# Part B's query, key and input turns moved to VectorE, with scores in eight 32x64 TensorE tiles

## The chip, the cores and the metric

The kernel runs on one core of a Trainium2 chip. The number that counts is the device time of one execution, in microseconds (us); it is given as the median of three runs. One further execution was taken with the hardware profiler, and all rows quoted below are from that one.

## The reference, cut to what matters

The program computes two independent parts and joins their outputs along the last axis. Part A is a sliding, dilated attention over 2048 tokens; the change does not touch its code. Part B is a recurrent attention: 2048 tokens are cut into 64 segments of 32, and each segment also reads 8 memory rows that the segment before it has written. So the 64 segments run strictly one after another.

```python
M, seg = (8, 32); H, Dh = (32, 192)
...
mem = mem0
for s in range(n_seg):                       # 64 segments
    xs = x[:, s * seg_len:(s + 1) * seg_len, :].copy()
    h = jnp.concatenate([mem, xs], axis=1)   # 40 rows of 640
    q = jnp.einsum('btd,dhe->bhte', h, Wq)   # k and v likewise
    ...
    scores = jnp.einsum('bhqe,bhke->bhqk', q, k) * scale
    scores = jnp.where(mask[None, None], scores, -1000000000.0)
    p = _softmax(scores, axis=-1)
    o = jnp.einsum('bhqk,bhke->bhqe', p, v)
    o = jnp.einsum('bhte,hed->btd', o, Wo)
    mem = o[:, :M, :].copy()
    outs.append(o[:, M:, :])
```

## The kernel before

Part A runs first, on all engines, for some 170 us. While it runs, SyncE's queue (SP, the one hardware DMA queue of the program) already loads a part of Part B's weights into SBUF, copies the rest into DRAM tiles in the form in which they will be streamed (`copy_streamed`), and copies the input x into a DRAM tile `xwindows`, 64 rows for each segment (`copy_windows`): 32 rows that the segment works on (the "main" rows: 8 memory rows and the first 24 tokens) and 32 rows "ahead", which hold the last 8 tokens of four neighbouring segments. These 8 last tokens need no memory, so their projections are made for four segments at once (`RENEW`, `turn_late`, the stored blocks `Lb`), one weight group at a time; a segment in which a group's turn comes makes two passes over its weights in place of one.

Part B's 32 heads are worked in four groups of 8 heads. For each of q, k and v and each group there are 1536 weight columns, and five row chunks of 128 rows (`dc`): one unit of 384 KB each. Wo is cut in 24 units of 320 KB. Most units stay in SBUF (`resident`); 24 of them (`STREAMED`: 8 of k, 6 of v, 10 of o) are fetched again in each segment from the DRAM copies, through a ring of six buffers (`wstream`).

A segment goes as follows on TensorE, whose order is written out by hand in `segment` (L659); ScalarE, VectorE and GpSimd are ordered by the scheduler of the tile layer:

- `project32` (L477): x is the stationary operand (128 rows by 32 tokens), weights stream past it, 384 columns in each of four column tiles of 32; five chunks give 20 matmuls in a pass.
- `to_sb` copies the 128x384 result from PSUM into SBUF as bf16. In it the partition holds a pair of heads and a token, and the columns hold the 384 features of the pair.
- `turn` (L495) turns it so that features lie on partitions: three 128x128 matmuls against the identity, into PSUM. `fill` then copies the result into `QT` or, in two halves, into `KT`, on ScalarE or VectorE. For the stored last tokens GpSimd copies from `Lb`.
- `scores` (L569): per group 16 matmuls of 128x64 (40 columns each) in two column tiles.
- `softmax`, `put_p`: VectorE and, for the exponential, ScalarE.
- `turn_p` (L603) turns the probabilities on TensorE, `mix` (L619) multiplies them with v in four row tiles of 32x128, 32 matmuls per group; four evacuations follow into `OT`.
- `project_out` (L633): 24 matmuls of 128x64 per group, 320 columns each, into `Y`.
- `memory_rows` (L645), at the segment's end: the 8 new memory rows of Y are turned on TensorE (after four `PAD` matmuls whose result is overwritten) and copied by VectorE into the x tile `HX` of the next segment.

x itself comes into `HX` by `load_x` (L467): one transposing DMA for each segment. PSUM has eight banks: three for `acc`, four for `ps_x` (turns, scores, mix), one for Y.

Of the kernel before, what the change touches and what calls it, by code (L numbers as in the profile page):

```python
# [7 lines left out]
FP32 = mybir.dt.float32  # L8
# [278 lines left out]
BLOCKS = 18  # L287
# [10 lines left out]
def part_b(ctx, tc, B_x, B_mem0, B_Wq, B_Wk, B_Wv, B_Wo, out, ident, n_seg, pre, nbuf, mid):  # L298
# [6 lines left out]
    w_in = {m: w.rearrange("(dc p) h e -> p dc (h e)", p=128) for m, w in (("q", B_Wq), ("k", B_Wk), ("v", B_Wv))}  # L305
# [4 lines left out]
    def unit_src(u):  # L310
        m, c, dc = u
        if m == "o":
            return wo_v[:, c]
        return w_in[m][:, dc, 1536 * c:1536 * c + 1536]
# [6 lines left out]
    def copy_streamed():  # L321

        order = [(m, g) for m, g in need]
        units = []
        for m, g in order:
            if m == "o":
                units += [("o", i, 0) for i in range(6 * g, 6 * g + 6) if i in STREAMED["o"]]
            else:
                units += [(m, g, dc) for dc in range(5) if m != "q" and dc in STREAMED[m][g]]
        for u in units:  # L330
            copied[u] = dpool.tile([128, unit_cols(u)], BF16, name="wcopy_%s%d_%d" % u)[:]
            nc.sync.dma_start(unit_tile(copied[u], u), unit_src(u))
# [19 lines left out]
    def load_resident(units, engs):  # L352
        for k, u in enumerate(units):
            engs[k % len(engs)].dma_start(unit_tile(res[u], u), unit_src(u))
# [8 lines left out]
    XW = dpool.tile([n_seg, 2 * SEG, Dm], BF16, name="xwindows")  # L363

    def copy_windows():

        rows = [(XW[0, 0:M], mem2[0:M]), (XW[0, M:SEG], x2[0:SEG - M])]
        for a, b in ((1, 49), (49, n_seg)):
            rows.append((XW[a:b, 0:SEG], x2[SEG * a - M:SEG * b - M].rearrange("(s n) d -> s n d", n=SEG)))
        groups = x2.rearrange("(t n) d -> t n d", n=SEG)[:, SEG - M:SEG]  # L370
        groups = groups.rearrange("(m k) n d -> k m n d", k=4)
        windows = XW[:].rearrange("(m k) n d -> k m n d", k=4)
        for r in range(4):
            for i in range(4):
                dst = windows[r][:, SEG + M * i:SEG + M * i + M]
                if i >= r:
                    rows.append((dst, groups[i]))
                else:
                    rows.append((dst[0:n_seg // 4 - 1], groups[i][1:n_seg // 4]))
                    rows.append((dst[n_seg // 4 - 1], groups[i][n_seg // 4 - 1]))  # L380
        for dst, src in rows:
            nc.sync.dma_start(dst, src)
# [14 lines left out]
    HXs = [xpool.tile([128, 5, 64], BF16, name=f"HX{i}") for i in range(2)]  # L397
# [5 lines left out]
    qk_sb = pool("b_qk", bufs=3)  # L403
# [3 lines left out]
    ps_x = pool("b_ps_x", bufs=4, space=PSUM)  # L407
# [32 lines left out]
    KT = cpool.tile([128, 4, 4, L], BF16, name="KT")  # L440
# [4 lines left out]
    free = [cpool.tile([128, 3, 4, M], BF16, name=f"Lb{i}") for i in range(BLOCKS)]  # L445
# [8 lines left out]
    for t in LV + [Vst]:  # L454
        nc.gpsimd.memset(t[:, 192:256], 0.0)

    copies = {"n": 0}
    S_, V_ = nc.scalar.copy, nc.vector.tensor_copy
    ENGINES = {"sb": {"q": (V_, S_, S_, S_), "k": (S_, S_, S_, S_)}, "late": (V_, V_, V_, V_),
               "QT": (S_, S_, S_, V_), "KT": (S_, S_, S_, S_), "V": (S_, V_, V_, S_), "LV": (V_, S_, S_, V_),  # L460
               "PT": (S_, V_, V_, V_)}

    def evacuate(dst, src):
        copies["n"] += 1
        (S_ if copies["n"] % 2 else V_)(dst, src)  # L465

    def load_x(s):  # L467
        if s < n_seg:
            nc.sync.dma_start_transpose(HXs[s % 2][:], XW[s])

    def main(s):
        return HXs[s % 2][:, :, 0:SEG]

    def ahead(s):
        return HXs[s % 2][:, :, SEG:2 * SEG]
# [19 lines left out]
    def turn(sb, chunks=(0, 1, 2)):  # L495
        pt = ps_x.tile([128, len(chunks), 4, 32], FP32, tag="x", name="pt")
        for k, c in enumerate(chunks):
            nc.tensor.matmul(pt[:, k], lhsT=sb[:, 128 * c:128 * c + 128], rhs=ident, start=True, stop=True)  # L498
        return pt

    def tokens(t):
        return t[:, 0:12 * L].rearrange("p (j c n) -> p j c n", c=3, n=L)

    def fill(copy, m, n0, n1, src):

        if m == "q":
            copy(tokens(QT)[:, :, :, n0:n1].rearrange("p j c n -> p c j n"), src)  # L507
            return
        fill_outer(copy, n0, n1, src[:, 0:3:2])
        fill_middle(copy, n0, n1, src[:, 1])  # L510

    def fill_outer(copy, n0, n1, src):
        copy(KT[:, :, 0:3:2, n0:n1].rearrange("p j c n -> p c j n"), src)  # L513

    def fill_middle(copy, n0, n1, src):
        copy(KT[0:64, :, 1, n0:n1], src[0:64])
        copy(KT[64:128, :, 3, n0:n1], src[64:128])  # L517

    def turn_late(sb, m, g, s, start):

        pt = turn(sb)
        for t in range(start, next_start(m, g, start)):
            rows = pt[:, :, :, M * (t % 4):M * (t % 4) + M]
            if t == s:
                if m == "k" and g == 0:
                    fill_middle(V_, 32, L, rows[:, 1])
                    fill_outer(S_, 32, L, rows[:, 0:3:2])
                else:
                    fill(S_, m, 32, L, rows)
            else:  # L530
                late[m, g, t] = free.pop(0)
                evacuate(late[m, g, t][:], rows)

    def project_qk(s, m, g):
        renew = s == 0 or f"{m}{g}" in RENEW[s % 4]
        Xs = [ahead(s), main(s)] if renew else [main(s)]
        ps = project32(Xs, m, g)
        sbs = [to_sb(p, c) for p, c in zip(ps, [ENGINES["late"][g], ENGINES["sb"][m][g]][2 - len(ps):])]

        def turn_ahead():  # L540
            if renew:
                turn_late(sbs[0], m, g, s, s)
            else:
                b = late.pop((m, g, s))
                fill(nc.gpsimd.tensor_copy, m, 32, L, b[:])
                free.append(b)

        def turn_main():
            if m == "k" and g == 0:
                fill_middle(V_, 0, 32, turn(sbs[-1], (1,))[:, 0])  # L550
                fill_outer(S_, 0, 32, turn(sbs[-1], (0, 2))[:])
            else:
                fill(ENGINES["QT" if m == "q" else "KT"][g], m, 0, 32, turn(sbs[-1])[:])

        return turn_ahead, turn_main
# [13 lines left out]
    def scores(g):  # L569
        Sps = ps_x.tile([128, 4, L], FP32, tag="x")  # L570
        for n in range(8):
            a, part = n // 2, n % 2
            for g2 in range(2):
                at = L * (3 * a + g2 + part)
                nc.tensor.matmul(Sps[64 * g2:64 * g2 + 64, a, :], lhsT=QT[:, at:at + 64],  # L575
                                 rhs=KT[:, a, ((0, 1), (3, 2))[g2][part], :], start=(n == 0), stop=(n == 7),
                                 tile_position=(0, 64 * g2))
        return Sps

    def softmax(Sps):  # L580
        t1 = one.tile([128, 4, L], FP32, tag="t1")
        nc.vector.scalar_tensor_tensor(out=t1[:], in0=Sps[:], scalar=scale,  # L582
# [20 lines left out]
    def turn_p(g):  # L603

        split = 2 if g == 3 else 1
        pt = ps_x.tile([128, 2, 128], FP32 if split > 1 else BF16, tag="x")
# [12 lines left out]
    def mix(g, PT):  # L619

        ps = [ps_x.tile([128, 3, L], FP32, tag="x", name=f"OTps{a}") for a in range(4)]
        plan = [(late, half, k, col) for late in range(2) for half in range(2)
                for k, col in (((0, 0), (1, 128)), ((2, 320), (1, 192)))[half]]
        for n, (late, half, k, col) in enumerate(plan):
            V = LV[g] if late else Vst
            for a in range(4):
                nc.tensor.matmul(ps[a][:, k, :], lhsT=V[32 * a:32 * a + 32, col:col + 128],  # L627
                                 rhs=PT[32 * a:32 * a + 32, late, half, :],
                                 start=(n == 0), stop=(n == len(plan) - 1), tile_position=(32 * a, 0))
        for a in range(4):  # L630
            evacuate(OT[:, 3 * L * a:3 * L * a + 3 * L], ps[a][:].rearrange("p k n -> p (k n)"))
# [13 lines left out]
    def memory_rows(s, Ysb):  # L645
        pt = ps_x.tile([128, 5, M], FP32, tag="x")
        for _ in range(PAD):
            nc.tensor.matmul(pt[:, 0, :], lhsT=ident, rhs=ident[:, 0:M], start=True, stop=True)
        for dc in (2, 0, 1, 3, 4):
            for gv in range(2):  # L650
                c0, c1 = max(128 * dc, 320 * gv), min(128 * dc + 128, 320 * gv + 320)
                if c0 < c1:
                    lo = c0 - 128 * dc
                    nc.tensor.matmul(pt[lo:lo + c1 - c0, dc, :], lhsT=Ysb[:, c0 - 320 * gv:c1 - 320 * gv],  # L654
                                     rhs=ident[:, 64 * gv:64 * gv + M], start=True, stop=True,
                                     tile_position=(0, lo))
        nc.vector.tensor_copy(HXs[(s + 1) % 2][:, :, 0:M], pt[:])  # L657

    def segment(s):  # L659
# [22 lines left out]
        both(tk[2])  # L682
        PT[1] = turn_p(1)
# [35 lines left out]
    load_x(0)  # L719
    for u in [(m, g, dc) for m, g in (("k", 0), ("k", 1), ("v", 0)) for dc in STREAMED[m][g]][:nbuf]:  # L720
        fetched[u] = fetch(u)
# [74 lines left out]
```

## Time and profile before

| | us |
|---|---|
| median of three runs | 1980.87 |
| lowest and highest run | 1975.70, 1982.82 |
| span of the profiled execution | 1976.8 |
| TensorE matmul busy | 1890.8 (96%) |
| VectorE busy | 1032.1 (52%) |
| ScalarE busy | 927.4 (47%) |
| GpSimd busy | 262.3 (13%) |
| SP's DMA queue, share of 16 engines' span | 91.3% |
| first matmul of Part B | 171.1 |

The busy times are sums over the whole program. A busy TensorE isn't one at its peak: the ends of matmuls are modelled, and overlapping matmuls in different tiles count once. The granted clock of TensorE was full (9 of 9 tenths shown) in all 40 slices. The profiled execution's span lies 4.1 us under the median of the runs and inside their spread of 7.1 us.

### The profile page before, as it was taken

How to read it: one execution, taken by the hardware profiler on the slowest of the kernel's cores; microseconds unless marked ns; L12 is line 12 of the kernel's file. 1: busy time of each engine (PE TensorE's matmuls, PEld its weight loads, DVE VectorE, ACT ScalarE, POOL GpSimd, SP SyncE). 2: the span in 40 equal slices, each digit the busy share in tenths (PEclk: the TensorE clock that was granted, in tenths of full speed). 3: DMA queues.
4: the chain of work that ended last, by engine and by line, in shares of the span. 5: the costliest groups of instructions: out<-in, count | busy, mean ns of one | idle time of the engine just before them, and what ended most of it. 6: DMA issues, size and time to landing. Idle time of an engine off the chain costs nothing.

```text
span 1976.8 us, 99618 instructions
## 1 busy us (share of the span) xinstructions
PE 1890.8 (96%) x43006; PEld 1221.6 (62%) x43006; DVE 1032.1 (52%) x3431; ACT 927.4 (47%) x2963; POOL 262.3 (13%) x1070
## 2 busy tenths in 40 slices
PE   8998899999999999999999999999999999999998
PEld 5665566666666666666666666666666666666665
DVE  4885454455444554455445554455445554555454
ACT  3554344444444454444444454444444444444443
POOL 2001011111111111111111111111111111111111
PEclk9999999999999999999999999999999999999999
DMA  9936999999999999999999999999999999999997
GB/s 332 298 111 227 341 324 312 327 326 326 324 321 324 322 328 315 329 319 331 326 318 322 329 330 314 325 315 316 327 328 324 327 327 315 338 325 329 315 328 262
DMA packets 278203, 621.62 MB, mean 314 GB/s; under 512 B 62089, under 2 KB 72329, under 8 KB 277449
## 3 DMA queue, kind: packets, MB, share of 16 engines
q1 hardware_dynamic: 272258, 609.17, 91.3%
q8 instruction: 337, 5.52, 1.1%
q0 software_dynamic: 5504, 6.07, 1.0%
q14 instruction: 104, 0.85, 0.1%
HBM read 602.01 MB, written 19.27 MB: 314 GB/s over the span
## 4 chain that ended last, share of the span: by engine, by line
PE 67%; DMA 17%; ACT 7%; DVE 6%; issue 2%; SPq 0%; ACTq 0%; POOL 0%; POOLq 0%; DVEq 0%
PE acc L485 31%; PE Y L641 17%; DMA t<-wcopy_k 7%; PE pt L498 7%; DMA t<-wcopy_o 6%; DMA t<-wcopy_v 4%; PE Sps L575 3%; PE pq L95 3%; PE OTps L627 3%; DVE prod L151 1%; ACT sb L712 1%; ACT OT L708 1%; PE pt L610 1%; ACT KT L513 1%; ACT t L588 1%
## 5 line engine op out<-in xcount | busy, mean ns | idle before, releaser
L485 PEld LDWEIGHTS <-HX 128*32 128x32 bf16 x19380 | 467.1, 96 | 283.8 <-issue 54.5
L641 PEld LDWEIGHTS <-OT 128*64 128x64 bf16 x6144 | 317.8, 110 | 137.0 <-ACT OT L465 25.0
L485 PE MATMUL acc<-t,HX 128*32 128x384 bf16 x4524 | 342.9, 328 | 19.0 <-DMA t<-wcopy_k 9.3
L641 PE MATMUL Y<-wres_o,OT 128*64 128x320 bf16 x3584 | 331.2, 302 | 9.9 <-DVE OT L465 5.1
L485 PE MATMUL acc<-wres_q,HX 128*32 128x384 bf16 x6460 | 333.6, 328 | 1.1 <-issue 0.7
L492 ACT CAST sb<-acc 128x384 bf16<-128x384 f32 x448 | 210.1, 478 | 152.0 <-PE acc L485 132.4
L641 PE MATMUL Y<-t,OT 128*64 128x320 bf16 x2560 | 266.7, 301 | 10.4 <-DMA t<-wcopy_o 8.8
L485 PE MATMUL acc<-wres_v,HX 128*32 128x384 bf16 x4520 | 251.7, 327 | 0.7 <-DMA wres_v<-in_B_Wv_dram 0.7
L485 PE MATMUL acc<-wres_k,HX 128*32 128x384 bf16 x3876 | 224.6, 327 | 0.3 <-DVE sb L492 0.3
L588 ACT ACTIVATE t<-t 128x160 f32<-128x160 f32 x256 | 86.4, 338 | 288.5 <-DVE t L587 284.5
L498 PE MATMUL pt<-ident,sb 128*128 128x128 bf16 x1938 | 182.4, 221 | 8.5 <-ACT KT L513 0.9
L582 DVE SCALAR_TENSOR_TENSOR t<-Sps,mask 128x160 f32<-128x160 f32 x256 | 82.9, 324 | 178.5 <-PE Sps L575 173.2
L465 ACT CAST OT<-OTps 128x120 bf16<-128x120 f32 x512 | 108.6, 266 | 140.4 <-PE OTps L627 139.2
L498 PEld LDWEIGHTS <-sb 128*128 128x128 bf16 x1938 | 109.4, 97 | 87.0 <-ACT sb L492 20.5
L590 DVE TENSOR_REDUCE sm<-t 128x4 f32<-128x160 f32 x256 | 82.0, 320 | 130.9 <-ACT t L588 130.9
L465 DVE CAST OT<-OTps 128x120 bf16<-128x120 f32 x512 | 123.7, 272 | 46.1 <-PE OTps L627 45.8
L513 ACT CAST KT<-pt 128x256 bf16<-128x256 f32 (+1 forms) x323 | 109.1, 343 | 78.6 <-PE pt L498 78.1
L517 POOL COPY KT<-Lb 64x32 bf16<-64x32 bf16 x189 | 40.0, 212 | 788.2 <-PE Sps L575 656.9
L575 PEld LDWEIGHTS <-QT 128*64 128x64 bf16 x4096 | 98.4, 112 | 59.1 <-issue 52.2
L575 PE MATMUL Sps<-KT,QT 128*64 128x40 bf16 x4096 | 113.9, 187 | 5.6 <-ACT QT L507 2.6
L657 DVE CAST HX<-pt 128x40 bf16<-128x40 f32 x63 | 12.6, 200 | 179.5 <-PE pt L654 179.5
L600 DVE TENSOR_TENSOR P<-t,sm 128x128 bf16<-128x128 f32 (+1 forms) x512 | 100.2, 237 | 11.2
(91 smaller groups left out, 2130.8 us busy)
## 6 DMA issues: line engine op xcount, KB each, us to landing
t<-wcopy_o SPq DMA_DIRECT2D x640, 320.0 KB, 4.9
t<-wcopy_k SPq DMA_DIRECT2D x512, 384.0 KB, 5.3
t<-wcopy_v SPq DMA_DIRECT2D x384, 384.0 KB, 5.3
wres_q<-in_B_Wq_dram SPq DMA_DIRECT2D x20, 384.0 KB, 7.8
wres_v<-in_B_Wv_dram SPq DMA_DIRECT2D x14, 384.0 KB, 7.9
wres_k<-in_B_Wk_dram SPq DMA_DIRECT2D x12, 384.0 KB, 7.8
wres_o<-in_B_Wo_dram SPq DMA_DIRECT2D x14, 320.0 KB, 7.1
wcopy_o<-in_B_Wo_dram SPq DMA_DIRECT2D x10, 320.0 KB, 9.6
```

Of the source, the lines that this page charges most:

```text
L95: nc.tensor.matmul(pq[32 * d:32 * d + 32], lhsT=wcol[:, k, t, 4 * c + d, :], rhs=xTs[s][:, k, :], start=(k == 0), stop=(k == 4), tile_posi ...
L465: (S_ if copies["n"] % 2 else V_)(dst, src)
L485: nc.tensor.matmul(ps[n][32 * j:32 * j + 32, :], lhsT=X[:, dc, :], rhs=w[:, 384 * j:384 * j + 384], start=(dc == 0), stop=(dc == 4), tile_ ...
L492: copy(sb[:], p[:])
L498: nc.tensor.matmul(pt[:, k], lhsT=sb[:, 128 * c:128 * c + 128], rhs=ident, start=True, stop=True)
L513: copy(KT[:, :, 0:3:2, n0:n1].rearrange("p j c n -> p c j n"), src)
L575: nc.tensor.matmul(Sps[64 * g2:64 * g2 + 64, a, :], lhsT=QT[:, at:at + 64], rhs=KT[:, a, ((0, 1), (3, 2))[g2][part], :], start=(n == 0), s ...
L582: nc.vector.scalar_tensor_tensor(out=t1[:], in0=Sps[:], scalar=scale, in1=mask[:].unsqueeze(1).to_broadcast([128, 4, L]), op0=ALU.mult, op ...
L588: nc.scalar.activation(t1[:], t1[:], ACTF.Exp)
L590: nc.vector.tensor_reduce(out=sm[:], in_=t1[:], axis=AX.X, op=ALU.add)
L600: nc.vector.tensor_tensor(out=P[:, k, :, at:at + hi - lo], in0=t1[:, :, lo:hi], in1=sm[:].unsqueeze(2).to_broadcast([128, 4, hi - lo]), op ...
L641: nc.tensor.matmul(Y[64 * gv:64 * gv + 64, :], lhsT=OT[:, L * c:L * c + 64], rhs=w[:, n:n + 320], start=(i == 0 and r == 0), stop=(i == 23 ...
```

## The change

Q, K and x are turned in 32x32 blocks by VectorE in place of whole turns by TensorE and the DMA. After a block turn, partition 32j+f holds feature f of a 32-feature block of head pair j, and the twelve blocks of the pair lie along the columns. So the scores' contraction runs over 32 partitions at a time: 48 matmuls per group in eight 32x64 tiles (four row tiles, two column tiles), and each row tile writes its own PSUM bank. `ps_x` becomes one buffer of four banks, shared by scores and mix; the turns of P and of the memory rows take their PSUM from the three `acc` banks.

x is copied in DRAM in quarter rows (160 columns), loaded by a plain DMA into `XS` and turned by VectorE (`turn_x`) into `HX`. This puts x's columns on partitions in another order (partition 32j+f of chunk dc holds column 160j+32dc+f), so the weight rows are loaded in that order too: four DMAs for a resident unit in place of one; the DRAM copies are reordered when they are made. `copy_windows` issues 104 DMAs in place of 26.

The copies out of PSUM for q, k, v and P all go to ScalarE; OT is evacuated by two instructions, one on each engine; the last 8 tokens go through VectorE's turn and a GpSimd copy; the buffers `sb` are two in place of three; the PAD matmuls are gone. The order of TensorE's work in `segment` stays, but for the turns of Q and K, which are no longer TensorE's.

```diff
-    w_in = {m: w.rearrange("(dc p) h e -> p dc (h e)", p=128) for m, w in (("q", B_Wq), ("k", B_Wk), ("v", B_Wv))}
+    w_in = {m: w.rearrange("(j dc f) h e -> dc f j (h e)", j=4, f=32) for m, w in (("q", B_Wq), ("k", B_Wk), ("v", B_Wv))}
...
+    def load_unit(eng, t, u):
+
+        if u[0] == "o":
+            eng.dma_start(unit_tile(t, u), unit_src(u))
+            return
+        for j in (0, 2, 1, 3):
+            eng.dma_start(t[32 * j:32 * j + 32, 0:unit_cols(u)], unit_src(u)[:, j])
...
-    XW = dpool.tile([n_seg, 2 * SEG, Dm], BF16, name="xwindows")
+    XW = dpool.tile([n_seg, 4, SEG, 2, 160], BF16, name="xwindows")
...
+        for j in range(4):
+            rows = [(XW[0, j, 0:M, 0], mj[j, 0:M]), (XW[0, j, M:SEG, 0], xj[j, 0:SEG - M])]
...
+            for dst, src in rows:
+                nc.sync.dma_start(dst, src)
...
-    qk_sb = pool("b_qk", bufs=3)
+    qk_sb = pool("b_qk", bufs=2)
...
-    ps_x = pool("b_ps_x", bufs=4, space=PSUM)
+    ps_x = pool("b_ps_x", bufs=1, space=PSUM)
...
+    ENGINES = {"sb": {"q": (S_, S_, S_, S_), "k": (S_, S_, S_, S_)}, "late": (S_, S_, S_, S_),
+               "V": (S_, S_, S_, S_), "LV": (S_, S_, S_, S_), "PT": (S_, S_, S_, S_)}
...
     def load_x(s):
         if s < n_seg:
-            nc.sync.dma_start_transpose(HXs[s % 2][:], XW[s])
+            nc.sync.dma_start(XS[:], XW[s].rearrange("j n w c -> (j n) (w c)"))
+
+    def turn_x(s):
+        if s < n_seg:
+            nc.vector.transpose(HXs[s % 2][:].rearrange("p w k n -> p (w k n)"), XS[:])
...
     def turn_late(sb, m, g, s, start):
 
-        pt = turn(sb)
+        lt = one.tile([128, 12, 32], BF16, tag="lt", name="lt")
+        nc.vector.transpose(lt[:], sb[:].rearrange("p (c n) -> p c n", n=32))
         for t in range(start, next_start(m, g, start)):
-            rows = pt[:, :, :, M * (t % 4):M * (t % 4) + M]
+            rows = lt[:, :, M * (t % 4):M * (t % 4) + M]
             if t == s:
...
+                nc.gpsimd.tensor_copy(tokens(m, 32, L), rows)
             else:
                 late[m, g, t] = free.pop(0)
-                evacuate(late[m, g, t][:], rows)
+                nc.gpsimd.tensor_copy(late[m, g, t][:], rows)
...
         def turn_main():
...
+            nc.vector.transpose(tokens(m, 0, 32), sbs[-1][:].rearrange("p (c n) -> p c n", n=32))
...
     def scores(g):
-        Sps = ps_x.tile([128, 4, L], FP32, tag="x")
-        for n in range(8):
...
+        Sps = ps_x.tile([128, 4, 512], FP32, tag="x")
+        for c in range(6):
+            for e in range(2):
+                for j in range(4):
+                    n = 6 * e + c
+                    nc.tensor.matmul(Sps[64 * e:64 * e + 64, j, 0:L], lhsT=QT[32 * j:32 * j + 32, L * n:L * n + 64],
+                                     rhs=KT[32 * j:32 * j + 32, n, :], start=(c == 0), stop=(c == 5),
+                                     tile_position=(32 * j, 64 * e))
...
     def mix(g, PT):
 
-        ps = [ps_x.tile([128, 3, L], FP32, tag="x", name=f"OTps{a}") for a in range(4)]
+        ps = ps_x.tile([128, 4, 512], FP32, tag="x", name="OTps")
...
-        for a in range(4):
-            evacuate(OT[:, 3 * L * a:3 * L * a + 3 * L], ps[a][:].rearrange("p k n -> p (k n)"))
+        for a, copy in ((0, S_), (2, V_)):
+            copy(OT[:, 3 * L * a:3 * L * a + 6 * L].rearrange("p (a n) -> p a n", a=2), ps[:, a:a + 2, 0:3 * L])
...
     def memory_rows(s, Ysb):
-        pt = ps_x.tile([128, 5, M], FP32, tag="x")
-        for _ in range(PAD):
-            nc.tensor.matmul(pt[:, 0, :], lhsT=ident, rhs=ident[:, 0:M], start=True, stop=True)
...
+        pt = ps_acc.tile([128, 5, M], FP32, tag="acc", name="mt")
+        for dc in range(5):
+            for j in range(4):
...
         values(s, 1)
         both(tk[2])
+        turn_x(s + 1)
         PT[1] = turn_p(1)
```

More of the change, by code (lines that the diff above doesn't have):

```diff
@@ L396, in part_b @@
     xpool = pool("b_hx", bufs=1)
-    HXs = [xpool.tile([128, 5, 64], BF16, name=f"HX{i}") for i in range(2)]
+    HXs = [xpool.tile([128, 2, 5, SEG], BF16, name=f"HX{i}") for i in range(2)]
+    XS = xpool.tile([128, 2 * 160], BF16, name="XS")
     wstream = pool("b_ws", bufs=nbuf)
@@ L493, in to_sb, with tokens @@
         return sb
[L495 to L517, printed above, removed]
+    def tokens(m, n0, n1):
+        return QT[:, 0:12 * L].rearrange("p (c n) -> p c n", n=L)[:, :, n0:n1] if m == "q" else KT[:, :, n0:n1]
     def turn_late(sb, m, g, s, start):
-        pt = turn(sb)
+        lt = one.tile([128, 12, 32], BF16, tag="lt", name="lt")
+        nc.vector.transpose(lt[:], sb[:].rearrange("p (c n) -> p c n", n=32))
         for t in range(start, next_start(m, g, start)):
-            rows = pt[:, :, :, M * (t % 4):M * (t % 4) + M]
+            rows = lt[:, :, M * (t % 4):M * (t % 4) + M]
             if t == s:
[L525 to L529, printed above, removed]
+                nc.gpsimd.tensor_copy(tokens(m, 32, L), rows)
             else:
                 late[m, g, t] = free.pop(0)
-                evacuate(late[m, g, t][:], rows)
+                nc.gpsimd.tensor_copy(late[m, g, t][:], rows)
     def project_qk(s, m, g):
@@ L605, in turn_p @@
         split = 2 if g == 3 else 1
-        pt = ps_x.tile([128, 2, 128], FP32 if split > 1 else BF16, tag="x")
+        pt = ps_acc.tile([128, 2, 128], FP32 if split > 1 else BF16, tag="acc", name="pt")
         for late in range(2):
```

85 lines of the change are left out of this document (32 added, 53 removed).

## The prediction

> **What bounds the kernel now.** I read the page's busy times first, then the chain that ended last (start us, length us, what) for one segment.
>
> ```profile
> PE 1890.8 (96%) x43006; PEld 1221.6 (62%) x43006; DVE 1032.1 (52%) x3431; ACT 927.4 (47%) x2963; POOL 262.3 (13%) x1070
> ```
> ```profile
> 1035.25 0.36 PE Sps L575 x16
> 1035.61 0.27 PE pt L498 x3
> ...
> 1038.04 0.93 PE acc L485 x20
> 1038.97 0.44 PE pt L498 x6
> ...
> 1039.52 1.75 PE Y L641 x24
> 1041.27 0.24 PE Sps L575 x16
> 1041.51 1.74 PE acc L485 x40
> 1043.25 0.31 PE OTps L627 x32
> ```
>
> TensorE works without a break, so a price per matmul can be read off. Two passes of 20 take 1.74 us, one takes 0.93: 0.81 for 20 more, and a fixed 0.12. Six turns take 0.44, three 0.27: 57 ns each, and a fixed 0.10. The 16 score matmuls take 0.36 behind a projection and 0.24 behind `project_out`, whose tiles have their form (128x64). So a change of tile form costs about 0.1 us, and I price it at 0.095. Mix gives 0.31 for 32, hence some 7 ns each beside the change; `project_out` 68 ns each.
>
> The second limit is the DMA. In windows of one segment (us, busy of PE, PEld, DVE, ACT, POOL, then granted clock, DMA share, GB/s):
>
> ```profile
> 996.00:997.00 1.00, 1.00 (x18) 0.80 (x15) 0.00 (x0) 0.00 (x0) 0.00 (x0) 1.00 2.15 243
> 997.00:998.00 1.00, 0.35 (x8) 0.14 (x3) 0.00 (x0) 0.00 (x0) 0.00 (x0) 1.00 0.56 55
> 998.00:999.00 1.00, 1.00 (x20) 0.45 (x17) 0.00 (x0) 0.66 (x2) 0.00 (x0) 1.00 0.52 126
> 999.00:1005.00 6.00, 5.59 (x127) 3.36 (x127) 1.94 (x7) 2.40 (x8) 0.98 (x2) 1.00 1.03 398
> ```
>
> The transposing load of x, issued at 993.6, empties the queue: three windows move 424 KB where the next ones move 398 in each, so it costs about 1.9 us of transfer. The streamed units are 8.78 MB a segment, 22.1 us at 398 GB/s; with the transposing load 24 of a segment's 27.9 (the copies of Y at L708 stand 27.9 apart). Waits on them reach TensorE (engine, line, waited for: total us, times, longest):
>
> ```profile
> PE acc L485 <- DMA t<-wcopy_k: 9.3, 19, 1.5
> PE Y L641 <- DMA t<-wcopy_o: 8.8, 23, 1.0
> PE acc L485 <- DMA t<-wcopy_v: 6.5, 13, 1.4
> ```
>
> **TensorE's own work, per segment.** Removed: 30 turns at 58 ns, 1.74 us; four PAD matmuls and six memory matmuls at about 26 ns, 0.26, against 20 new ones at 12 (four column tiles side by side, as in a projection), 0.24. Changes of tile form: 28 before, 24 after by the order of the built program, 0.38 less; the scores lose their free transition from `project_out`, which that count holds. Scores: 64 matmuls at 15.6 ns, 1.00 us. After, 192 matmuls in 24 rounds of eight tiles. Before, a round of two tiles takes 0.24/8 = 30 ns, and in mix a round of four (0.31-0.09)/8 = 27; so the round didn't grow with its tiles. The lower bound is 28 ns a round, 0.17 us a group; the upper one has no overlap at all, 48 x 15 ns = 0.72. At mix's price for each matmul it would be 0.33. I take 36 ns a round, 0.22 a group, 0.86 a segment, near the lower end, since two and four tiles cost the same. Sum: -1.74 - 0.02 - 0.38 - 0.14 = -2.28 us.
>
> **What the turns had covered.** TensorE did the turns while VectorE and ScalarE worked on a softmax; VectorE now does them, in the middle of that softmax. Its turn of 128x384 is in no row. The same shape cast costs 554 ns, its fixed share being 175 (the four-element reciprocal):
>
> ```profile
> L492 DVE CAST sb<-acc 128x384 bf16<-128x384 f32 x135 | 74.8, 554 | 48.3 <-PE acc L485 46.0 <-PE pt L498 2.2
> L151 DVE TENSOR_TENSOR prod<-VT,Pr 128x2048 bf16<-128x2048 bf16 x40 | 47.2, 1218 | 4.9 <-ACT Pr L147 4.9
> L134 DVE TENSOR_REDUCE sm<-ex 128x64 f32<-128x512 f32 x8 | 8.4, 1046 | 0.7 <-ACT ex L129 0.7
> ```
>
> Scaled to 384 elements, L151 gives 0.37 us (the lower bound), L134 0.83 (the upper one). I take 0.55, by the row of the same shape. [...]
>
> I followed VectorE's new order through the first half of a segment. *First chain:* after `scores(0)` it does the scaling, the turn of q1, the maximum, the turn of k1, the subtraction; ScalarE's exponential follows, behind the copy of q2; then sum, reciprocal and P. In the trace the softmax alone runs from 1035.65 to 1038.18, 2.53 us. Each turn adds 0.3: of its 0.55, 0.1 overlaps the next instruction, and it fills the pauses between dependent ones. With 0.23 until VectorE sees the last matmul, `turn_p(0)` can start 3.35 us after the scores. TensorE's own work up to there is q2, v0 and `scores(1)`, with changes 2.15. It waits 1.2 us, and 0.4 in the quarter of the segments where v0 has two passes: on average 1.0. *Second chain*, from P(0) to P(1): softmax 2.5, turns of q2 and k2 0.3 each, half of OT 0.3, together 3.4 us; TensorE does `turn_p(0)`, k2, `mix(0)`, v1, 2.3 us. It waits 1.1 us, which a second pass of k2 or v1 covers in half of the segments; the average is 0.6. `scores(1)` waits 0.6 us where k1 has two passes and 0.1 in another, on average 0.17. `project_out(Y, 2)` waits 0.3, since the turn of x stands ahead of half of OT on VectorE; mix(3) 0.1. At the segment's end TensorE waits 0.33 for Y's copy and 0.45 for the new memory rows, with no turns to fill the second. Sum 2.93. The same walk over the old order gives 0.88 (0.3 of it at the end). So new waits take 2.05 us of the 2.28. What is queued behind the waiting instruction: `turn_p` holds k2 or `project_out`, and these hold the buffers that SP refills, but the DMA has slack by then. GpSimd's copies of the last tokens (0.26 us each, two to five in a row) run beside VectorE's turns and end before `scores` in that walk; ScalarE loses the fills of QT and KT (323 us by its rows at L507, L513, L516 and L517, 5.0 a segment) and gains some 3 us of copies (sb, V, P), so these cost nothing, except where one stands ahead of an exponential, which the chains hold. Two `sb` buffers, one four-bank `ps_x` and three `acc` banks for more uses add no wait in that walk: each is read out before its turn comes again.
>
> **DMA.** The plain load of 80 KB takes about 0.2 us at 398 GB/s, and it leaves 22.3 us of transfers in a segment of 27. I take the waits of TensorE for DMAs as gone: 9.3 + 8.8 + 6.5 and 2.2 for the first segment's units, 27 us.
>
> **The start of Part B.** SP's rows now:
>
> ```profile
> 93.47 22.70 SPq L382 DMA_DIRECT2D xwindows<-in_B_x_dram  x25
> ...
> 117.53 30.67 SPq L417 DMA_DIRECT2D t<-wcopy_k  x4
> ```
>
> 104 issues at the median of 0.587 us are 61 us, and four DMAs for a resident unit of q, k or v add about 8 us ahead of them: `copy_windows` ends near 163 in place of 116. Queued behind it are x's first load, the first streamed units and 36 small loads. The idle 30 us (SP waited for Part A's buffers in L417) take most of it. I allow 6 us of delay; 0 if the issues take 0.4, 25 if the quarter rows land slowly.
>
> **Sum.** 63 segments x (-2.28 + 2.05) = -15; DMA -27; start +6: -36. From the span of 1976.8 that is 1941; the median of the runs stands 4 above that span, so the forecast for it is 1945.
>
> **Rivals.** *A, score tiles don't overlap* (slower). If 32x64 tiles go out at the price of a single old score matmul, 15 ns, a group costs 0.72, 2.0 us a segment more, of which some 1.5 isn't absorbed by the chains: 1945 + 94 = 2039. It decides from 11 ns a matmul on, where the gain is spent. For it: no row shows eight tiles. Against it: mix at 7. [...] *B, VectorE's turn is dear* (slower): at 0.8 us, near L134, the two chains and the two exposed late turns cost 1.3 us a segment more, 1945 + 82 = 2027; from about 0.70 on the gain is spent. *C, the freed time goes nowhere* (same): the next stream wait or instruction supply (TensorE's weight loads wait "issue" 52 us at L575 and 61 at L627, short matmuls both, and there will be more of these) takes the 36 us: 1981. *D, cheap turns* (faster): at 0.37 the chains shrink by 0.5 us: 1913.
>
> **Numbers.** Forecast 0.53, D 0.12, A 0.13, B 0.12, C 0.10. About 0.5% is what a measurement can tell from no change, 10 us. The forecast's own spread is 1915 to 1970, so it and D are faster: 0.64 after a hundredth lost at its edge; same 0.11; slower 0.25. For 8 in 10 the range runs from 1890 (D with scores at the lower bound) to 2015 (A or B at half their price with a late start).
>
> **What would show it.** Right: `turn_p` waits for VectorE about 1.6 us a segment and the memory rows about 0.8; turns near 0.55 us; 48 score matmuls in some 0.22 beside the change of form; no dip of the DMA rate at x's load; first matmul of Part B near 177. Wrong: score blocks over 0.5 us, turns over 0.7, or waits for streamed weights that stay.

## The result and the profile after

The changed kernel takes 2172.59 us, the median of four runs (2170.21 to 2174.96), where the kernel before takes 1979.49 on the same chip: a ratio of 1.098, 95% interval 1.096 to 1.101. The forecast was 1945, and the range ended at 2015. The profiled execution has a span of 2168.7 us against 1976.8, 191.9 more.

First the page: busy times, then three rows of the span in 40 slices (busy share of TensorE, its granted clock, busy share of the DMA engines, in tenths), then a queue that brings instructions (packets, MB, share of 16 engines).

```profile
PE 1849.8 (85%) x49890; PEld 1138.9 (53%) x49890; DVE 1021.2 (47%) x2946; ACT 768.1 (35%) x1964; POOL 315.5 (15%) x1216
...
PE   8398688898888988888988888888898889888887
...
PEclk9699799999999999999999999999999999999999
DMA  7864899889998898899888988999898888889997
...
q8 instruction: 391, 6.41, 1.2%
```

TensorE was busy 96% of the span and is busy 85%. It isn't that another engine took over: VectorE and ScalarE are at a smaller share than before, and so is SP's DMA queue (85.0% for 91.3%). The instruction queue has 391 packets where it had 337. TensorE has more matmuls (49890 for 43006), yet fewer busy us, and 319 us in which it does nothing. Slices 2 and 5 of the PE row (3 and 6 tenths) show that some of that lies at the start.

Two numbers divide the 191.9 us. ScalarE comes to its copy of Y to `OT` once in each segment: every 27.87 us before and every 30.04 us now, 63 x 2.17 = 137 us. It comes to the first one at 268.7 us in place of 213.4: 55 us. (It then still waits for Y: the copies themselves start at 272.1 in place of 217.5 and stand 30.01 and 27.83 apart, which divides the time in the same way. All segment times and first copies below are counted like the first pair.)

**Inside a segment.** The chain that ended last (start us, length us, what), around two groups of scores of one segment:

```profile
1051.16 0.48 PE Sps L558 x48
1051.64 1.74 PE acc L496 x40
1053.38 0.42 PE Sps L558 x40
1053.80 2.93 issue
1056.73 0.23 PE Sps L558 x8
...
1058.41 3.32 PE acc L496 x20
```

The 48 score matmuls at 1051.16 take 0.48 us. The next 48 are broken off after 40, and for 2.93 us TensorE waits for nothing that the profile shows. Operands can't be the reason: the eight matmuls that are left belong to the tile that the forty before them worked on. The DMA view of just that gap:

```profile
q1 hardware_dynamic: 405, 1.06, 95.5%
q8 instruction: 1, 0.02, 2.0%
```

One packet of the instruction queue moves in it, 16 KB, while the streams have the DMA engines to 95.5%. By the packet's own record it starts at 1054.53, 0.73 us after the matmuls stopped, takes 0.94 and lands at 1055.47; the matmuls go on 1.26 us later. In b1 below, 128 matmuls more in each of the 64 segments, with as many weight loads, bring 64 packets more (401 for 337), so one packet for 256 TensorE instructions, a block; the changed kernel's 13768 TensorE instructions more (matmuls and weight loads by the pages) come with 54 packets more. From 290 us on, 134 pairs of neighbouring matmuls of the same line start more than 0.6 us apart, and the second one starts 1.39 us after the nearest landing of such a packet (median; 90% of them 1.23 to 1.59). From this I take it that TensorE had run out of instructions. Before, there were 36 such pairs, spread from -2.2 to 2.0 us (90% of them). In the band of 1.15 to 1.7 us lie 131 of the 134, but only 15 of the 36: some blocks were late before, too.

The last piece shown costs again: two passes of a projection, 40 matmuls, in 3.32 us, where those at 1051.64 took 1.74. (The chain counts 20, since the matmuls there start two at a time by the profile; the window below holds 42, the two behind them included.) The same stretch in windows (us, busy of PE, PEld, DVE, ACT, POOL, granted clock, DMA share, GB/s):

```profile
1051.50:1053.20 1.70, 1.70 (x55) 1.01 (x45) 1.48 (x5) 0.67 (x2) 0.48 (x2) 1.00 1.00 303
1053.80:1056.70 2.90, 0.00 (x0) 0.00 (x0) 0.89 (x4) 0.36 (x1) 0.00 (x0) 1.00 0.98 371
1058.41:1061.73 3.32, 3.32 (x42) 1.38 (x42) 1.59 (x6) 1.02 (x4) 0.00 (x0) 0.51 0.98 311
```

The granted clock is 0.51 in it, right after the gap. From 290 us to the last matmul, half clock makes up 92 us of the changed kernel and nothing of the one before.

Over all of Part B, TensorE's weight loads wait (engine, line, waited for: total us, times, longest):

```profile
PEld L496 <- issue: 150.0, 264, 3.6
PEld L558 <- issue: 109.5, 270, 3.2
PEld L610 <- issue: 80.6, 216, 1.7
PEld L593 <- DVE P L583: 65.9, 95, 1.7
```

Only the last of these four is a wait that the prediction had priced. The other three are not late blocks throughout: without streams (d1 below) 23.8, 65.0 and 57.5 us of them stay.

**At the start.** SP's issues in the changed kernel (start us, length us, engine, line, operation):

```profile
89.14 3.20 SPq L49 DMA_TRANSPOSE xT<-in_A_x_dram  x1
...
185.64 19.27 SPq L394 DMA_DIRECT2D xwindows<-in_B_x_dram  x25
205.02 0.52 SPq L476 DMA_DIRECT2D XS<-xwindows  x1
```

Part A's third block of x (L49) is asked for at 89.1 us, where it was 51.7 before: it stands behind the four-fold loads of the resident units (L322, 132 of them where there were 33), which run from 17.4 us on. TensorE idles from 59.4 to 94.4 us for it. The window copies then run until 205 us, and Part B's first x and its first streamed units come behind them.

### The profile page after: what moved, and what is told of

Read it like the earlier page. It is cut to its first block, busy times and chain, and to the rows that moved or that the text cites. A ratio compares the mean times of both kernels' runs of the same rounds, so it can differ in the third digit from the quotient of the medians.

```text
span 2168.7 us, 112058 instructions
## 1 busy us (share of the span) xinstructions
PE 1849.8 (85%) x49890; PEld 1138.9 (53%) x49890; DVE 1021.2 (47%) x2946; ACT 768.1 (35%) x1964; POOL 315.5 (15%) x1216
## 4 chain that ended last, share of the span: by engine, by line
PE 67%; DVE 11%; issue 10%; DMA 4%; SPq 4%; ACT 4%; POOL 0%; ACTq 0%; POOLq 0%; DVEq 0%
PE acc L496 33%; PE Y L624 19%; PE Sps L558 5%; SPq L322 3%; PE OTps L610 3%; PE pt L593 2%; PE pq L95 2%; DVE KT L536 1%; DVE sm L573 1%; ACT OT L688 1%; DVE P L583 1%; ACT t L571 1%; DMA t<-wcopy_v 1%; DVE OT L614 1%; PE po L161 1%
## 5 line engine op out<-in xcount | busy, mean ns | idle before, releaser
L532 POOL COPY QT<-Lb 128x96 bf16<-128x96 bf16 x252 | 67.6, 268 | 886.9 <-PE Sps L558 858.4
L558 PE MATMUL Sps<-KT,QT 32*64 32x40 bf16 x12288 | 146.5, 191 | 42.3 <-issue 38.0
L558 PEld LDWEIGHTS <-QT 32*64 32x64 bf16 x12288 | 116.4, 104 | 123.2 <-issue 109.5
L536 DVE STREAM_TRANSPOSE QT<-sb 128x384 bf16<-128x384 bf16 x256 | 144.7, 565 | 67.2 <-ACT sb L503 67.2
L614 DVE CAST OT<-OTps 128x240 bf16<-128x240 f32 x256 | 101.0, 395 | 156.4 <-ACT OT L614 156.1
L536 DVE STREAM_TRANSPOSE KT<-sb 128x384 bf16<-128x384 bf16 x256 | 144.7, 565 | 42.9 <-ACT sb L503 42.8
L550 ACT CAST Vst<-acc 128x384 bf16<-128x384 f32 x256 | 122.2, 478 | 91.2 <-PE acc L496 90.2
L95 PE MATMUL pq<-xT,a_wq 128*32 128x512 bf16 x1200 | 80.6, 404 | 38.6 <-DMA xT<-in_A_x_dram 35.0
L614 ACT CAST OT<-OTps 128x240 bf16<-128x240 f32 x256 | 91.1, 356 | 62.9 <-PE OTps L610 62.9
L519 POOL COPY Lb<-lt 128x96 bf16<-128x96 bf16 x453 | 101.6, 268 | 65.0 <-DVE lt L512 64.9
```

The costliest lines, as they stand in the source:

```text
L95: nc.tensor.matmul(pq[32 * d:32 * d + 32], lhsT=wcol[:, k, t, 4 * c + d, :], rhs=xTs[s][:, k, :], start=(k == 0), stop=(k == 4), tile_posi ...
L519: nc.gpsimd.tensor_copy(late[m, g, t][:], rows)
L536: nc.vector.transpose(tokens(m, 0, 32), sbs[-1][:].rearrange("p (c n) -> p c n", n=32))
L550: copy(w, p[:].rearrange("p (h e) -> p h e", h=2))
L558: nc.tensor.matmul(Sps[64 * e:64 * e + 64, j, 0:L], lhsT=QT[32 * j:32 * j + 32, L * n:L * n + 64], rhs=KT[32 * j:32 * j + 32, n, :], start ...
L614: copy(OT[:, 3 * L * a:3 * L * a + 6 * L].rearrange("p (a n) -> p a n", a=2), ps[:, a:a + 2, 0:3 * L])
```

## The experiments

Theory: while the weight streams run, a block of 256 instructions comes late, and a kernel with more short matmuls uses its blocks up faster than they come; the start is late by SP's queue. Rivals: the new matmuls cost more by themselves; the waits for VectorE cost more than reckoned; the streams slow every kernel alike.

### The start: a1, a4

a1 puts the third block of x ahead after 14 units and gives half of the window copies to GpSimd:

```diff
-        load_resident(resident[:n_pre], [nc.sync])
+        load_resident(resident[:14], [nc.sync])
         turn_x(2)
+        load_resident(resident[14:n_pre], [nc.sync])
...
+        copy_windows((0, 1), nc.gpsimd)
+        return lambda: copy_windows((2, 3), nc.sync)
```

> The changed kernel, with Part A's third x load put ahead of most resident weight loads on SP, and half of the window copies issued by GpSimd while it is idle. Theory 1 (the 55 us that Part B starts late come from SP's 104 window copies at 0.75 us each and from x's third load standing behind 128 small loads): first copy of Y near 222 us in place of 269, whole time 2172 - 45 = 2127. Rival (the transfers themselves are slow, wherever they are issued): first copy of Y stays above 255, time 2160 or more. In both the segments stay at 30.0 us.

Measured: 2162.53 us (1.094 of before, 1.088 to 1.101); first matmul of Part B at 202.5 us, first copy of Y at 248.4, segments of 30.25. The copies' share is seen (first matmul to first Y 45.9 us, 60.7 in the changed kernel, 42.3 before), the rest not: GpSimd's issues now stood ahead of Part A's masks, which came at 49.5 us, and TensorE idled there instead. A miss in the edit, so the first part was tried in another way. a4 leaves SP's order as it is and loads each resident unit of q, k and v by one DMA:

```diff
...
-        for j in (0, 2, 1, 3):
-            eng.dma_start(t[32 * j:32 * j + 32, 0:unit_cols(u)], unit_src(u)[:, j])
+        m, c, dc = u
+        eng.dma_start(t[:, 0:1536], w_plain[m][:, dc, 1536 * c:1536 * c + 1536])
```

> The changed kernel with one DMA in place of four for each resident unit of q, k and v (their rows then stand in the old order, so Part B's values are other ones; the work is the same). Theory 1 (the start is late because Part A's third and fourth blocks of x stand behind the four-fold DMAs in SP's queue): the third block is asked for at about 52 us again, TensorE's 35 us of idling are gone, first matmul of Part B at 171 to 180 (208 in the changed kernel), first copy of Y at 225 to 245 (268.7), 2125 to 2150 in all, segments as they are at 30.0. Rival (the start is late by the DMA work, not by the issues, or by the window copies alone): first matmul at 200 or later, 2165 or more in all.

Measured: 2122.05 us (1.073, 1.066 to 1.080); segments 29.95. SP's rows of a4:

```profile
51.36 6.54 SPq L49 DMA_TRANSPOSE xT<-in_A_x_dram  x1
...
172.04 0.52 SPq L478 DMA_DIRECT2D XS<-xwindows  x1
```

The third block is asked for at 51.4 us again, the first matmul of Part B is at 174.7 and the first copy of Y at 220.1. The window copies end at 172. So 48.6 of the 55 us go with the four-fold loads. The 6.7 that are left I put down to the copies; no run changed these alone. The total is 3 us better than expected.

### More matmuls, with and without streams: b1, b2, d0, d3, d1

b1 is the kernel before with 128 unread mix matmuls a segment (`range(8)`), b2 with 256 (`range(16)`):

```diff
+        for n in range(8):
+            for a in range(4):
+                nc.tensor.matmul(ps[a][:, 3, :], lhsT=Vst[32 * a:32 * a + 32, 0:128],
+                                 rhs=PT[32 * a:32 * a + 32, 0, 0, :], start=True, stop=True,
+                                 tile_position=(32 * a, 0))
...
```

> The kernel before, with 32 more matmuls of mix's form ahead of each mix, into a PSUM column that nothing reads: 256 instructions more a segment, 1600 in place of 1344, and nothing else. Theory 1 (instruction supply): the gaps marked issue appear in the old kernel too, 60 to 190 us of them beside the price of 59 us (128 matmuls at 7.2 ns in 64 segments), time 2100 to 2230, with stretches of half clock. Theory 2 (gaps are a by-product of VectorE's turns and the new buffers): price alone, 1980 + 59 = 2040, clock full.

> The kernel before with 64 more matmuls in each mix, whose results nobody reads: 256 matmuls, 512 instructions more in a segment, 1856 in all, 7.25 blocks of 256 (6.25 with half as many, which took 31.35 us a segment). Theory 1 (supply, about 5.0 us a block): 36.2 us a segment, 2430 to 2510 in all. Theory 2 (each matmul costs what it costs in the trace of before, 7.2 ns, and the 31.35 with half as many came from something else that doesn't grow): 29.7 us a segment by the price alone or 32.3 with that same addition, 2095 to 2260 in all.

d1, d0 and d3 take away the streams from the changed kernel, from the kernel before and from b1; resident weights of the same shape stand in for the streamed ones:

```diff
-        return fetch(u)
+        return get_unit(("o", 0, 0) if u[0] == "o" else (u[0], u[1], 1))
...
-    for u in [(m, g, dc) for m, g in (("k", 0), ("k", 1), ("v", 0)) for dc in STREAMED[m][g]][:nbuf]:
-        fetched[u] = fetch(u)
```

> The changed kernel with no streamed weights in the segments: where a streamed unit is needed, a resident unit of the same kind is read in its place, so the DMA is nearly idle and TensorE's instructions are the same. Theory 1a (the instruction blocks are late because they queue behind the weight streams on the same DMA engines): gaps go, time 1990 to 2020 (the late start stays). Theory 1b (TensorE's own prefetch is the limit, whatever the DMA does): gaps stay, time 2130 to 2160, less only the 35 us that TensorE waits for streamed weights. Theory 2 gives the same as 1b.

> The kernel before without streamed weights: what it would stream is taken from resident weights of the same shape. Theory 1 (weight streams make the instruction blocks late, and before has few short matmuls enough that little of this shows): its 27 us of DMA waits and part of its 49 us of gaps go, 27.2 to 27.6 us a segment (27.87 with streams), 1935 to 1960 in all. Theory 2 (streams slow every kernel's TensorE by the same 3 us a segment that the changed kernel lost when it had them, 30.04 against 26.98): 24.8 us a segment, 1785 in all.

> The kernel before with 128 unread mix matmuls a segment, and without streamed weights: the fourth corner beside before, the same matmuls with streams (31.35 us a segment) and no streams without them. Theory 1 (blocks of instructions come late only under the streams): the 128 matmuls cost about their price of 0.92 us, 28.0 to 28.7 us a segment, 1990 to 2035 in all. Theory 2 (the matmuls cost 3.3 us by themselves, streams or not): 30.6 to 31.0, 2150 to 2180 in all.

Measured, us for a segment, with the total and its ratio to the kernel before:

| | TensorE instructions a segment | with streams | without |
|---|---|---|---|
| before | 1276 | 27.87 | 26.93 (d0: 1913.45, 0.968 [0.964, 0.971]) |
| 128 more matmuls | 1532 | 31.35 (b1: 2192.37, 1.109 [1.105, 1.113]) | 28.26 (d3: 1996.35, 1.009 [1.007, 1.012]) |
| 256 more matmuls | 1788 | 34.55 (b2: 2402.90, 1.215 [1.208, 1.223]) | |
| changed kernel | 1492 | 30.04 | 26.98 (d1: 1961.14, 0.992 [0.989, 0.995]) |

The instructions are matmuls and weight loads, counted in Part B's segments. The expectations have 68 more in each case, since they divide the whole program's matmuls by 64, Part A's among them; the differences are the same.

The 128 matmuls cost 1.33 us without streams and 3.48 with them; their price was 0.92. The change costs 0.05 us without streams and 2.17 with them. Neither the matmuls nor the new waits make the kernel slow by themselves, and the streams alone don't either: before loses 0.94 to them, 59 us in all. It is both together. The pairs in the band behind a packet go with the streams: 15 before, 91 in b1 and 131 in the changed kernel; none in d0, none in d3, one in d1. The chain of b1, where line 632 is the unread matmuls, and of d3, with the same program but for the streams:

```profile
1016.55 0.14 PE OTps L632 x14
1016.69 0.94 issue
1017.63 0.29 PE OTps L632 x18
```

```profile
1016.01 0.29 PE OTps L632 x32
```

With streams the matmuls stop in the middle of a series that needs nothing new; without, all 32 go out in 0.29 us. b1 and d3 are in the brackets of late blocks; d1 is on that side too, but 29 us under the bracket: the changed kernel loses more to its streams than I had thought. b2 is between its two expectations, nearer to the first: 34.55 us for 7.0 blocks are 4.9 each, where b1 has 5.2 (31.35 for 6.0), so the rate isn't fixed, as I had taken it to be; a block more cost 3.48 us the first time and 3.20 the second. d0's 1913.45 is 21 us under its bracket: before too loses more to its streams than its visible DMA waits, 25 us.

The change adds 216 instructions to a segment, 0.84 of a block; at 3.2 to 3.5 us a block that is 2.7 to 2.9 us. The 2.17 measured are less, which is plausible, since part of the new matmuls' own time is in that price and the turns' time is gone; I did not separate these.

### Fewer score matmuls, half the streams, fewer buffers: a2, d2, a3

a2 leaves out 24 of the 48 score matmuls of a group (`range(3)` for `range(6)`, with `stop` at the third), so half of the scores' contraction:

> The changed kernel with three of the six 32-feature chunks of each score left out (24 score matmuls a group in place of 48; the contraction is cut in half). Theory 1 (TensorE runs out of instructions: they come in blocks of 256, and 1560 a segment, in dense stretches, outrun the supply): with 1368 a segment, near the 1344 of before, most gaps marked issue and most of the half clock go, time 1975 to 2020. Theory 2 (the time is the price of the score matmuls, 7.8 ns each, and VectorE's chains): 96 matmuls at 7.8 ns are 0.75 us a segment, 48 us in all, time 2125; the gaps stay.

Measured: 2032.33 us (1.028, 1.025 to 1.031), some 12 us above the first theory's bracket; segments of 27.88, 2.16 us less for 192 instructions (0.75 of a block). By their price they'd be worth 0.75. So again three quarters of a block are worth over two us.

d2 takes every second streamed unit of the changed kernel from resident weights:

```diff
...
-        return fetch(u)
+        count.append(u)
+        return fetch(u) if len(count) % 2 else get_unit(("o", 0, 0) if u[0] == "o" else (u[0], u[1], 1))
```

> The changed kernel with every second streamed unit taken from resident weights: 12 loads of 320 or 384 KB a segment in place of 24. Theory 1a (a block's delay grows with the traffic): segments between 26.98 and 30.04, 28.0 to 28.9 us, 2040 to 2095 in all. Theory 1b (what counts is whether a load is on its way when a block is asked for, and with half the loads most blocks find none): 27.0 to 27.8 us, 1975 to 2030. Theory 1c (any stream at all does it): 29.5 to 30.0, 2135 to 2170.

Measured: 1998.14 us (1.010, 1.007 to 1.013), segments of 27.30, in the bracket of theory 1b: taking away half of the streams wins back 2.74 of the 3.06 us. Its DMA queue shows what is left, 57.4% of the engines in place of 85.0:

```profile
q1 hardware_dynamic: 167924, 333.49, 57.4%
```

So the loss isn't in proportion to the traffic; most of it comes between 57% and 85% of the DMA engines. The instruction packets say the same. Counted from the execution of the same instruction of the program (one in 256), a packet starts 0.69 us later with half of the streams than with none, and 2.20 us later with all (medians), while the packet itself takes some 1 us in each (medians 1.12, 0.96 and 0.95). Whether a block then finds no load on its way, as 1b has it, I did not look at.

a3 gives the changed kernel four stream buffers in place of six (`nbuf=4`):

> The changed kernel with four buffers for streamed weights in place of six, so that fewer of their transfers are queued when an instruction block is asked for. Theory 1a (an instruction block waits behind the transfers that are queued on the same DMA engines): fewer or shorter gaps that end behind a block, 28.5 to 29.5 us a segment, 2080 to 2140 in all. Theory 1b (the block is slowed by the traffic as a whole, not by the queue's depth): gaps as they are and more waits for weights, 30 to 31 us a segment, 2170 to 2230 in all.

Measured: 2310.14 us (1.168, 1.162 to 1.174), segments of 32.23: outside both brackets. Its waits of TensorE's matmuls:

```profile
PE Y L624 <- DMA t<-wcopy_o: 113.6, 162, 2.5
PE acc L496 <- DMA t<-wcopy_v: 90.0, 119, 14.4
```

With four buffers the weights themselves come late, and there are more pairs of matmuls over 0.6 us apart (335 from 290 us on, the waits for weights among them, for 200). Those of one line in the band behind a packet are fewer, 67 for 131. That can be the shorter queue's doing, or that of the waits for weights, in which the instructions catch up; the run doesn't decide it.

### The x part: h1, e1

h1 is the kernel before with the x part alone: plain loads, VectorE's turn in place in `HX`, reordered weight rows. The window copies, the start and the memory rows change with it; these are the main lines of the edit:

```diff
-            nc.sync.dma_start_transpose(HXs[s % 2][:], XW[s])
+            nc.sync.dma_start(HXs[s % 2][:].rearrange("p w k n -> p (w k n)"), XW[s].rearrange("j n w c -> (j n) (w c)"))
+
+    def turn_x(s):
+        if s < n_seg:
+            v = HXs[s % 2][:].rearrange("p w k n -> p (w k n)")
+            nc.vector.transpose(v, v)
```

> The kernel before with the x part alone: plain loads of x in quarter rows, turned by VectorE in place, weight rows reordered, the 20 matmuls of the memory rows and the PAD kept; Q, K, the turns by TensorE and the scores as before. Three quarters of the window copies are issued by GpSimd at the end of Part A, and x's block 2 is loaded after ten resident units. TensorE's instructions in a segment: 1372 (1344 before, 1560 after), 5.36 blocks of 256. Theory 1 (the supply of instruction blocks, about 5.0 to 5.3 us a block while weights stream, bounds the segment): 27.2 to 28.0 us a segment, so the gain of the DMA waits that the prediction named (27 us) is mostly kept, and the total is 1945 to 1990 with a start of Part B that is 0 to 20 us later. Theory 2 (the x part itself, by its small loads and the VectorE turn of x, makes the segment dear): 29 us a segment or more, 2050 or more in all.

Measured: 2265.19 us (1.147, 1.139 to 1.155), segments of 31.84. That is the bracket of theory 2, but not by its mechanism:

```profile
DVE HX L489 <- DMA HX<-xwindows: 214.7, 62, 5.7
```

VectorE stands 3.5 us in a segment in front of its turn, with the evacuations of `OT` queued behind it, until x lands. The changed kernel has a buffer of its own, `XS`, which is free early, and waits 18.6 us in all at that place (three times). My variant without `XS` made the load late, so it is no test of the x part; what it shows is what the work queued behind a step pays when the step stands ahead of its data.

e1 tests the step on DMA waits alone, on the kernel before with only the first two of its 64 transposing loads (`if s < 2`):

> The kernel before with only the first two of its 64 transposing loads of x (the later segments work on the values of these; the work of the engines is the same). The prediction's step: while such a load runs the streams nearly stand still, so TensorE's waits for streamed weights, 25 us, are its doing; then they go here, 27.4 to 27.5 us a segment, 1945 to 1955 in all. Rival (the waits come from the streams themselves, which are 85 to 90 per cent of what the DMA engines can carry): waits of 18 us or more stay, 27.7 to 27.9 us a segment, 1965 to 1980.

Measured: 1964.49 us (0.994, 0.992 to 0.997), segments of 27.66. Waits of TensorE for streamed weights in e1:

```profile
PE Y L641 <- DMA t<-wcopy_o: 8.1, 21, 1.3
PE acc L485 <- DMA t<-wcopy_v: 4.2, 11, 0.7
```

With 0.8 for k, 13.1 us are left of 24.6. The time, too, ended between the two brackets, nearer to the rival's. Half of these waits were the transposing load's doing, half the streams' own.

No kernel that computes the whole result beat the kernel before.

## Why the prediction was wrong, step by step

The account below is per segment of 290 to 1850 us, by the time from each matmul's start to the next one's, which is counted to the work of the second (us):

| | before, no streams | changed, no streams | before | changed |
|---|---|---|---|---|
| projections | 12.14 | 12.52 | 12.65 | 14.55 |
| turns of Q and K | 2.82 | 0 | 2.83 | 0 |
| scores | 1.94 | 2.53 | 1.96 | 3.23 |
| turns of P, with waits | 0.70 | 2.37 | 0.69 | 1.95 |
| mix | 1.78 | 1.78 | 1.94 | 2.24 |
| `project_out` | 6.89 | 7.25 | 7.14 | 7.54 |
| memory rows | 0.67 | 0.53 | 0.67 | 0.53 |
| sum | 26.93 | 26.98 | 27.87 | 30.04 |

- **The step that failed: "63 segments x (-2.28 + 2.05)", and rival C's price.** The prediction took what TensorE executes and what it waits for as the whole of a segment, and priced the supply of instructions at 36 us at most, as a place where a gain goes, not as a cost that grows with the count: 1492 instructions a segment for 1276. Rival C (chance 0.10) named it, and sent the reader to the "issue" waits at L575 and L627. Those rows were something else: without streams, where no series breaks off behind a packet, they stand nearly unchanged in the kernel before (d0: 50.7 and 57.7 us, none longer than 0.5), so I take them mostly for changes of tile form. The sign of a late block is not their sum but their longest wait (0.5 us at d0's scores and 1.1 at d1's, 3.2 at the changed kernel's) and the stop within a series. The two right-hand columns against the two on the left show the cost: 0.94 us before, 3.06 after, most of it in the projections (2.0 us) and the scores (0.7), part of it as half clock. This term, (3.06 - 0.94) x 63 = 134 us, is what the forecast lacked in the segments. Without streams no gap in a series ends in the band behind a packet in d0 or d3, and one does in d1; with the data queue at 85.0% of the DMA engines 131 do. The rows of d0:

```profile
PEld L627 <- issue: 57.7, 208, 0.3
PEld L575 <- issue: 50.7, 145, 0.5
```

- **Start, "about 8 us" for the four-fold loads.** The mis-sized term. They delayed not only what lies behind in SP's queue, but Part A's own block of x, which the prediction didn't list among what they are moved past; it is asked for 37 us later, and 48.6 us of the start go with the four-fold loads (a4). For the other half, the window copies, the delay came out right, 6.7 us for 6, but in part by luck: the 104 copies take 78 us where 61 were said, and in a4, without the four-fold loads, they end at 172 where 163 was said with them. The first matmul of Part B is at 174.7 (177 was said). How the rest of the copies' time was hidden is not shown.
- **Scores, 0.86 us a segment.** Too low: 48 take 0.48 us in the chain, and without streams the 192 take 1.44 us within their series, 7.7 ns each, 0.39 more than the old 64. It is mix's price, the one that the prediction named and passed over, because two tiles and four had cost the same per round; eight did not. That costs 0.5 us a segment, 33 us of forecast. Rival A (15 ns, 0.72 us a group) is refuted by these 0.48: eight tiles do overlap.
- **VectorE's turn, 0.55 us.** Right: 565 ns.

```profile
L536 DVE STREAM_TRANSPOSE QT<-sb 128x384 bf16<-128x384 bf16 x256 | 144.7, 565 | 67.2 <-ACT sb L503 67.2
```

Rivals B (0.8) and D (0.37) fall.
- **New waits, 2.05 us.** Right where they can be seen alone: without streams the turns of P take 1.67 us more (1.6 was said), `project_out` 0.36 more (0.3). In the changed kernel itself the first is 1.26, probably since the gaps let VectorE catch up. (The prediction's terms add up to 2.95, not 2.93.)
- **Sum of a segment, -0.23.** Measured without streams: +0.05. The walk through the engines was sound to 0.3 us. The scores alone are 0.53 worse, so the rest came out some 0.25 better than forecast, which no run divides.
- **DMA waits gone, 27 us.** As a row this came true: beside one wait of 14.4 us at the start, 5.7 us remain. As a gain it did not: TensorE is late for other reasons and finds its weights there. And e1 shows that the cause named for them, the transposing load, was only half of it: 12 us to be had.

Together: 55 us of start where 6 were forecast, and 137 in the segments where a gain of 15 and of 27 by DMA waits was.

## What to carry to other kernels

Count the instructions of the busiest engine as a cost of their own where the DMA engines are nearly full (91.3% and 85.0% by the queue of data transfers before and after): here each 256 more on TensorE cost 3.2 to 3.5 us a segment beside weight streams (b1, b2), and 1.3 without (d3). Replacing few large matmuls by many small ones cost 0.05 us a segment without streams (d1) and was paid for a second time beside them, 2.17. And look at what is queued behind every DMA that becomes four, in the part of the program that issues it, not only in the part that it serves: here that was 48.6 us (a4).

## What was not expected of the hardware

- The packet of a block of instructions starts 2.20 us later (median) with the changed kernel's streams, where the queue of data transfers runs at 85.0%, than without them (d1), and 0.69 later at 57.4% (d2); the packet itself takes 0.95 to 1.12 us (medians) in all three, so it is its start that moves. Why it starts late is not shown; shortening the stream queue (a3) didn't answer it.
- In the changed kernel's profile half clock follows idling that is not long. It comes in pieces of 3.41 us: from 290 us on there are 25 of that length or its double, and a last one behind its last matmul. I count as idle the time between the starts of neighbouring matmuls where that is over 0.4 us. The 3.41 us ahead of the 25 pieces hold 1.74 us or more of it in 24 cases and 1.47 in one; among 466 such stretches ahead of full clock none holds over 2.10 us.
- Eight 32x64 tiles over four banks issue at 7.7 ns a matmul (d1), close to the 6.5 ns within a series of mix's four row tiles of 32x128 (before and after), so the price here goes by the matmul and not by the round.
